# Sliding-window attention feeding a SwiGLU block: key blocks of 64 with four TensorE tiles, against key blocks of 32 with eight

## The chip, the cores and the metric

The kernel runs on one core of a Trainium2 chip. The metric is device time in microseconds (us) for one execution of the whole program. Three runs of the kernel before took 326.04, 326.06 and 326.34 us; the median is 326.06 us.

Engine names follow the profile. PE is TensorE, and PEld is its weight load, which is an instruction of its own ahead of each matmul. DVE is VectorE, ACT is ScalarE, POOL is GpSimd and SP is SyncE. SP and POOL here also issue DMAs.

## The reference

Queries, keys and values are (8 batches, 8 heads, 576 positions, 64 wide). Every query sees itself and the 63 keys before it.

```python
rel = pos[:, None] - pos[None, :]
mask = (rel >= 0) & (rel < 64)
scores = np.where(mask, q @ k.T / 8, -1e9)
attn = softmax(scores)                       # over keys
x = (attn @ v)                               # heads side by side: 4608 tokens x 512
g = x @ w_gate                               # 512 x 1536
out = (g * sigmoid(g) * (x @ w_val)) @ w_out # 1536 x 512
```

The output is 4608 x 512 in float32.

## The kernel before, in words

The 4608 tokens are taken in nine tiles of 512. Tiles 0 to 6 and 8 are the first 512 positions of one batch each; tile 7 (`LAST`) is the last 64 positions of all eight batches. The order of the instructions on each engine is written out by hand, and each engine runs its own list in that order.

One tile has two parts. The attention part gives `xT`, the block's input with the 512 features on partitions. The feed-forward part is 12 gate and value steps (`gate_value`, matmuls on L429) and 4 output projections of 12 matmuls (`project_part`, L438). A gate step is 4 + 4 matmuls of 128x512 into two PSUM banks, a Silu on ACT (L422) and a multiply on DVE (L423) that gives a slice of `hT`. The gate bank alternates between banks 4 and 5, the value bank between 6 and 7, and three `sg` buffers stand between ACT and DVE. The projections of tile t-1 are interleaved with the attention of tile t (main loop at the end of the kernel), so PE has dense work while ACT and DVE handle the attention's softmax.

The attention of a tile from tile 1 on:

- `scores(t, w)` (matmuls on L269) handles four heads, w = 0 or 1. A key block of 64 keys meets the queries of its own block and of the next one, 128 in all. Heads lie as pairs; the half h of the pair is on partitions 64h to 64h+63 (contraction over 64), and the pair x of the two is written to PSUM partitions 64x to 64x+63. So four matmuls, (h, x), use four 64x64 quarters of the PE array. One call makes 32 matmuls: 28 with 128 columns and 4 with 64. In tile 7 a block meets only 64 columns and the call makes 64 matmuls.
- After it, for each h: an exponential on ACT (L282, 960 columns), a multiply by the 0/1 `mask` on DVE (L285), and an addition of the two blocks that one query sees (L290), which gives `both`.
- `sums` (matmuls in `totals`, L302) sums the weights with a matrix of ones, 4 matmuls of 512 columns per w, and ACT takes the reciprocal as exp(-log) (L316, L319).
- `mix` (L369) multiplies values with weights: again 32 matmuls per w in four quarters, 64 in tile 7. `scale` (L385) multiplies by the reciprocal and writes `xT`.

Between these visits PE does projections: visit 1 is `scores(t, 0)`, visit 2 is `scores(t, 1)` with the first `sums`, visit 3 is the second `sums` with `mix`.

Queries and keys come by DMA from POOL (`load_q`, 4 DMAs a tile, 16 in tile 7; `load_k`, 16 DMAs), two tiles ahead of use; values by SP into `v_f`, cast by POOL (`cast_v`). The last tile's values (`load_last_v`, 16 DMAs from POOL) are issued in tile 6. DVE turns queries and keys into the layout with features on partitions (`turn_q` L207, `turn_k` L217) behind gate steps 1, 4, 7 and 10 (6, 7, 9 and 10 in tile 1).

Of the kernel before, what the change touches and what calls it, by code (L numbers as in the profile page):

```python
# [8 lines left out]
P = 128  # L9
# [8 lines left out]
def kernel(  # L18
# [36 lines left out]
    vl = v12[:].rearrange("r g i (c w h) d -> r (g i) c w h d", c=2, w=2)  # L55
    vb = [cst.tile([P, 8, 2, 2, D], BF16, name=f"vb{i}") for i in range(2)]
# [6 lines left out]
    mask = cst.tile([P, 8, 2, 16, 4], BF16, name="mask")  # L63
# [20 lines left out]
    def load_q(t):  # L84

        w = 16 * D - 32
        q_s = stage.tile([P, 4, 16 * D], BF16, name="q_s", tag="q")
        for a, c in quarters:
            p0 = 64 * a + 32 * c
            if t != LAST:  # L90
                nc.gpsimd.dma_start(  # L91
                    q_s[p0:p0 + 32, :, 0:w],
                    q[batch(t), a:H:2, 0:512].rearrange("u (r e) d -> r u (e d)", e=16)
                    [:, :, 32 * c:32 * c + w],
                )
            else:
                for u in range(4):
                    nc.gpsimd.dma_start(  # L98
                        q_s[p0:p0 + 32, u, 0:w],
                        q[:, 2 * u + a, 512:576].rearrange("b (r e) d -> b r (e d)", e=16)  # L100
                        [:, :, 32 * c:32 * c + w],
                    )
        return q_s
# [44 lines left out]
    def load_halves(eng, dst, t, hds=range(H)):  # L148

        for hd in hds:  # L150
            w, x, h = hd // 4, hd // 2 % 2, hd % 2
            eng.dma_start(  # L152
                dst[64 * x:64 * x + 64, :, w, h],
                v[batch(t), hd, 0:512].rearrange("(j r) d -> r j d", r=64),
            )

    def load_last_v():
        for c in range(2):
            for hd in range(H):
                w, x, h = hd // 4, hd // 2 % 2, hd % 2  # L160
                s0 = S - P + 64 * c
                nc.gpsimd.dma_start(
                    vl[64 * x:64 * x + 64, :, c, w, h],
                    v[:, hd, s0:s0 + 64].rearrange("b r d -> r b d"),
                )

    def new_v(t):
        staged[t, "v"] = stage.tile([P, 8, 2, 2, D], FP32, name="v_f", tag="v", bufs=1)

    def stage_v(t):  # L170
        new_v(t)
        load_halves(nc.sync, staged[t, "v"], t)

    def cast_v(t):
        for i in range(4):
            js = slice(2 * i, 2 * i + 2)
            nc.gpsimd.tensor_copy(vb[t % 2][:, js], staged[t, "v"][:, js])  # L177
# [34 lines left out]
    def turn(t, u):  # L212
        turn_q(t, u)
        turn_k(kT[t % 2], staged[t][1], u)

# [31 lines left out]
    quadrants = [(x, h) for h in range(2) for x in range(2)]  # L247

# [3 lines left out]
    def scores(t, w):  # L252

        qT = queries[t]
        s_ps = wide(), wide()
        for j in range(8):
            if t == LAST:
                k_j = kT[t % 2 if j < 4 else 2]
                pieces = [(j, j + 1, 0, k_j, P * (j % 4) + 64),
                          (j, j + 1, 1, k_j, P * (j % 4))]  # L260
            else:
                pieces = [(j, min(8, j + 2), 0, kT[t % 2], 64 * j)]
            for lo, hi, c, src, k0 in pieces:
                for h in range(2):
                    for x in range(2):
                        slot = s_ps[h][half(x)].rearrange("r a b -> r (a b)")
                        n = hi - lo
                        o = P * j + 64 * c
                        nc.tensor.matmul(  # L269
                            slot[:, o:o + 64 * n].rearrange(  # L270
                                "r (n e y) -> r e n y", n=n, e=16
                            ),
                            src[half(h), 2 * w + x, k0:k0 + 64],
                            blocks(qT[half(h), 2 * w + x], t, lo, hi).rearrange(
                                "r e (n y) -> r e n y", n=n
                            ),
                        )
        n = 1024 if t == LAST else 960
        for h in range(2):
            E = eb[2 * w + h]  # L280
            flat = E[:].rearrange("r s z -> r (s z)")[:, 64:64 + n]
            nc.scalar.activation(  # L282
                flat, s_ps[h][:].rearrange("r a b -> r (a b)")[:, 0:n], AF.Exp, scale=0.125
            )
            nc.vector.tensor_mul(  # L285
                flat, flat, mask[:].rearrange("r j c e y -> r (j c e y)")[:, 0:n]
            )
            both = epool.tile([P, 8, 64], BF16, name="both", tag="both")
            lo = 2 if t == LAST else 0
            nc.vector.tensor_add(both[:], E[:, 1:17:2], E[:, lo:lo + 15:2])  # L290
            weights[t, w, h] = E, both
# [7 lines left out]
    def totals(t, w, d):  # L299
        for h in range(2):  # L300
            for x in range(2):
# [3 lines left out]
                    weights[t, w, h][1][half(x)].rearrange("r j (e y) -> r j e y", e=16),  # L305
# [4 lines left out]

    def turned(ap):

        return ap.rearrange("r (e x) -> r x e", e=16)
# [7 lines left out]
    def sums(t, w):  # L321
        d = d_tile(), d_tile()
        totals(t, w, d)
        for x in range(2):
            r = room(1)[:, 0]
            if t == NT - 1:
                log(r.rearrange("r (x e) -> r x e", e=16), turned(d[x]))
            else:
                log(r, d[x])
            invert(r)  # L330
            inverse[t, 2 * w + x] = r

    def sums_wide(t, w):
        d_ps, r = wide(), room(2)
        totals(t, w, (d_ps[:, 0], d_ps[:, 1]))
        for x in range(2):
            inverse[t, 2 * w + x] = r[:, x]
        log(r, d_ps[:])
        invert(r)

# [17 lines left out]
    def mix(t, w, o):  # L358
        E = [weights.pop((t, w, h))[0] for h in range(2)]
        for j in range(8) if t == LAST else (0, 2, 4, 6, 1, 3, 5, 7):  # L360
            if t == LAST:
                pieces = [(j, j + 1, 2 * j + 1 + c, vl[:, j, 1 - c]) for c in range(2)]
            else:
                pieces = [(j, min(8, j + 2), 2 * j + 1, vb[t % 2][:, j])]
            for lo, hi, s0, src in pieces:
                n = hi - lo
                for h in range(2):
                    for x in range(2):
                        nc.tensor.matmul(  # L369
                            blocks(o[x][half(h)], t, lo, hi).rearrange(  # L370
                                "r e (n y) -> r n e y", n=n
                            ),
                            src[half(x), w, h],
                            E[h][half(x), s0:s0 + n].rearrange("r n (e y) -> r n e y", e=16),
                            start=lo == 0 and s0 == 1, stop=lo == 7 and (t != LAST or s0 == 16),
                        )

    def scale(t, u, o_ps):
# [3 lines left out]
        if t == NT - 1:  # L382
            x, o_ps = x.rearrange("r (x e) -> r x e", e=16), turned(o_ps)
            r = r.rearrange("r (x e) -> r x e", e=16)
        nc.vector.tensor_mul(x, o_ps, r)  # L385

    taken = {"a": 0, "g": 0, "v": 0}

    def take(tag):
        taken[tag] += 1  # L390
        return taken[tag] % 2 ^ 1

    def wide():
        return two[take("a")]

    def d_tile():
        return bank[6 + take("v")]

    def mix_all(t):
        tiles = wide(), wide()  # L400
        for w in range(2):
            mix(t, w, (tiles[w][:, 0], tiles[w][:, 1]))
        for u in range(4):
            scale(t, u, tiles[u // 2][:, u % 2])
# [8 lines left out]

    def gate_tiles():
        return out_tile(), d_tile()
# [9 lines left out]
    def gate_value(t, m):  # L425
        pair = gate_tiles()
        for ps, w in zip(pair, (wg, wv)):
            for c in range(4):
                nc.tensor.matmul(  # L429
                    ps[:], w[:, c, P * m:P * m + P], xT[t][:, c, :],  # L430
                    start=(c == 0), stop=(c == 3),
                )
# [10 lines left out]
    def project_end(t, s, o_ps, copy=nc.vector.tensor_copy):  # L443
# [14 lines left out]
        if t == LAST:  # L458
            rows = out.rearrange("(b s) f -> b s f", s=S)[:, 512:S]
            rows = rows.rearrange("b (r e) f -> e b r f", e=16)  # L460
        else:
            rows = rows.rearrange("(r e) f -> e r f", e=16)
        for i in range(4):
            nc.sync.dma_start(rows[4 * s + i], os_[32 * i:32 * i + 32])

    def out_tile():
        return bank[4 + take("g")]

    def project(t, s):
        o_ps = out_tile()  # L470
        project_part(t, (s,), (o_ps,), range(12))
        project_end(t, s, o_ps)

    def project_last(t, s):
        r0 = S * batch(t) + P * s
        os_ = fsb.tile([P, 512], FP32, name="os_", tag="os_", bufs=4)
        for f0, f1 in ((0, 384), (384, 512)):
            o_ps = out_tile()
# [165 lines left out]
    taken["g"] = taken["v"] = 1  # L644
# [38 lines left out]
    tiles = [out_tile(), d_tile(), out_tile(), d_tile()]  # L683
# [5 lines left out]
    scores(1, 0)  # L689
    columns(1, 4)  # L690
    scores(1, 1)
# [81 lines left out]
```

## Time and profile before

| | before |
|---|---|
| median of 3 runs | 326.06 us (326.04 to 326.34) |
| the profiled execution: its own time | 326.34 us |
| its span from first to last instruction | 324.4 us |
| PE busy | 315.9 us, 97% of the span |
| DVE busy | 217.8 us, 67% |
| ACT busy | 167.0 us, 51% |
| POOL busy | 146.3 us, 45% |
| granted TensorE clock | 1.0 |

Busy time is the union of an engine's instructions. Matmuls overlap: a 128x512 matmul lasts 379 ns, but the next one starts about 216 ns later, so the mean duration of one is not its price. The price is the distance between starts, which the chain of waits gives (the stretch of a run of matmuls divided by their number). A few records of matmuls can be missing; the chain then shows an "issue" gap of 0.05 us where nothing stood still.

### The profile page before, as it was taken

Reading aid. Unit: us, or ns where it says so; the run is one execution under the profiler, and the core shown is the slowest. Engines: PE = TensorE matmul, PEld = TensorE weight load, DVE = VectorE, ACT = ScalarE, POOL = GpSimd, SP = SyncE. Lnnn points to the kernel's source line nnn. Section 1 sums busy time; section 2 is a strip of 40 time slices with the busy share of each in tenths; the row PEclk is TensorE's granted clock in tenths of the full one; section 3 lists DMA queues with packets and bytes.
Section 4 is the critical chain, followed back from the end, with each engine's and each line's share of the span. In section 5 each row is a group of like instructions: output and inputs, shape, how many; then the busy total and the mean of one; then the engine's idle time right before and its main releaser. Section 6 shows DMA issues by size and latency. Waiting matters only on the chain.

```text
span 324.4 us, 7013 instructions
## 1 busy us (share of the span) xinstructions
PE 315.9 (97%) x2737; PEld 150.9 (47%) x2780; DVE 217.8 (67%) x345; ACT 167.0 (51%) x239; POOL 146.3 (45%) x260
## 2 busy tenths in 40 slices
PE   7999999999999999999999999999999999999996
PEld 3644444444444444445444544444444544444443
DVE  4764756398676776887678766876687576774422
ACT  5952766337633683358336743565347633773310
POOL 4964766965085794576224999363200000000000
PEclk9999999999999999999999999999999999999999
DMA  7999999998889999949922999599501400021013
GB/s 254 201 196 199 207 154 189 173 172 99 170 156 198 135 171 186 193 58 223 200 34 32 167 182 97 42 197 190 99 3 34 99 2 0 10 85 40 0 25 105
DMA packets 83521, 40.35 MB, mean 124 GB/s; under 512 B 64160, under 2 KB 78752, under 8 KB 83488
## 3 DMA queue, kind: packets, MB, share of 16 engines
q0 software_dynamic: 51488, 22.59, 58.1%
q1 hardware_dynamic: 31456, 16.79, 21.4%
q10 hardware_dynamic: 544, 0.52, 0.5%
q8 instruction: 21, 0.34, 0.4%
q14 instruction: 12, 0.10, 0.1%
HBM read 53.02 MB, written 9.44 MB: 193 GB/s over the span
## 4 chain that ended last, share of the span: by engine, by line
PE 86%; issue 1%; DVE 0%
PE one L429 51%; PE one L438 28%; PE two L269 3%; PE two L369 2%; PE one L302 1%; PE one L480 1%; PE two L302 0%; DVE os__4138 L484 0%
## 5 line engine op out<-in xcount | busy, mean ns | idle before, releaser
L422 ACT ACTIVATE sg<-one 128x512 f32<-128x512 f32 x107 | 63.9, 597 | 112.5 <-PE one L429 86.3
L423 DVE TENSOR_TENSOR hT<-sg,one 128x512 bf16<-128x512 f32 x107 | 74.1, 693 | 60.7 <-PE one L429 59.8
L429 PE MATMUL one<-xT,wg 128*128 128x512 bf16 x414 | 108.1, 379 | 0.9
L429 PE MATMUL one<-xT,wv 128*128 128x512 bf16 x416 | 107.3, 379 | 0.1
L438 PE MATMUL one<-wo,hT 128*128 128x512 bf16 x396 | 93.7, 380 | 2.0 <-issue 0.5
L126 POOL DMA_DIRECT2D k_s<-in_k_dram x112 | 60.7, 567 | 25.0 <-DMA q_s<-in_q_dram 18.1
L429 PEld LDWEIGHTS <-wv 128*128 128x128 bf16 x424 | 41.5, 98 | 50.0
L429 PEld LDWEIGHTS <-wg 128*128 128x128 bf16 x424 | 41.3, 98 | 49.9 <-issue 0.3
L438 PEld LDWEIGHTS <-hT 128*128 128x128 bf16 x420 | 39.0, 98 | 46.6 <-issue 1.8
L282 ACT ACTIVATE eb<-two 128x960 bf16<-128x960 f32 (+1 forms) x32 | 29.5, 974 | 16.5 <-PE two L269 16.4
L217 DVE STREAM_TRANSPOSE kT<-k_s 128x512 bf16<-128x512 bf16 x28 | 36.0, 1286 | 0.0
L285 DVE TENSOR_TENSOR eb<-eb,mask 128x960 bf16<-128x960 bf16 (+1 forms) x32 | 21.1, 659 | 13.0 <-ACT eb L282 13.0
L177 POOL CAST vb<-v_f 128x512 bf16<-128x512 f32 x20 | 11.5, 627 | 34.9 <-DMA out_dram<-os__1184 12.4
L385 DVE TENSOR_TENSOR xT<-two,r 128x512 bf16<-128x512 f32 x34 | 21.7, 685 | 5.7 <-PE two L369 4.8
L319 ACT ACTIVATE r<-r 128x512 f32<-128x512 f32 (+1 forms) x34 | 22.3, 655 | 1.0
L207 DVE STREAM_TRANSPOSE qT<-q_s 128x512 bf16<-128x512 bf16 x32 | 22.2, 700 | 0.2
L316 ACT ACTIVATE r<-one 128x512 f32<-128x512 f32 x31 | 18.3, 591 | 4.7 <-PE one L302 4.7
L91 POOL DMA_DIRECT2D q_s<-in_q_dram x24 | 13.0, 564 | 5.4 <-DVE qT L207 5.4
L290 DVE TENSOR_TENSOR both<-eb 128x512 bf16<-128x512 bf16 x32 | 13.6, 425 | 1.1
L488 ACT ACT_TABLE_LOAD x9 | 11.5, 1283 | 2.0 <-issue 1.9
L152 POOL DMA_DIRECT2D vb<-in_v_dram x16 | 11.3, 723 | 1.9 <-DMA wo<-in_moe_w_out_dram 1.4
L98 POOL DMA_DIRECT2D q_s<-in_q_dram x16 | 8.6, 631 | 7.1 <-DVE qT L207 7.1
(119 smaller groups left out, 191.7 us busy)
## 6 DMA issues: line engine op xcount, KB each, us to landing
k_s<-in_k_dram POOLq DMA_DIRECT2D x112, 56.0 KB, 4.5
q_s<-in_q_dram POOLq DMA_DIRECT2D x24, 248.0 KB, 5.7
v_f<-in_v_dram SPq DMA_DIRECT2D x40, 128.0 KB
wg<-in_moe_w_gate_dram POOLq DMA_DIRECT2D x5, 256.0 KB, 8.1
wv<-in_moe_w_val_dram POOLq DMA_DIRECT2D x5, 256.0 KB, 8.7
q_f<-in_q_dram SPq DMA_DIRECT2D x4, 256.0 KB
wo<-in_moe_w_out_dram POOLq DMA_DIRECT2D x2, 512.0 KB, 9.3
vb<-in_v_dram POOLq DMA_DIRECT2D x16, 64.0 KB, 4.1
```

Of the source, the lines that this page charges most:

```text
L126: nc.gpsimd.dma_start(k_s[p0:p0 + 32, g, :, 0:w], k[b, a:H:2, s:s + P].rearrange("u (r e) d -> r u (e d)", e=4) [:, :, 32 * c:32 * c + w],)
L207: nc.vector.transpose(queries[t][:, u, :].rearrange("r (e x) -> r e x", e=16), staged[t][0][:, u].rearrange("r (e d) -> r e d", d=D)[:, :, ...
L217: nc.vector.transpose(dst[:, u, :].rearrange("r (g x e) -> r g e x", g=4, e=4), k_s[:, :, u].rearrange("r g (e d) -> r g e d", d=D)[:, :, ...
L282: nc.scalar.activation(flat, s_ps[h][:].rearrange("r a b -> r (a b)")[:, 0:n], AF.Exp, scale=0.125)
L285: nc.vector.tensor_mul(flat, flat, mask[:].rearrange("r j c e y -> r (j c e y)")[:, 0:n])
L316: nc.scalar.activation(r, d_ps, AF.Ln)
L319: nc.scalar.activation(r, r, AF.Exp, scale=-1.0)
L385: nc.vector.tensor_mul(x, o_ps, r)
L422: nc.scalar.activation(sg[:], g_ps[:], AF.Silu)
L423: nc.vector.tensor_mul(hT[t][:, m, :], sg[:], v_ps[:])
L429: nc.tensor.matmul(ps[:], w[:, c, P * m:P * m + P], xT[t][:, c, :], start=(c == 0), stop=(c == 3),)
L438: nc.tensor.matmul(o_ps[:], hT[t][:, c, P * s:P * s + P], wo[:, c, :], start=(c == 0), stop=(c == 11),)
```

## The change

Tiles 0 and 1 keep the old scheme (the functions are renamed `scores_second`, `sums_second`, `mix_second`). From tile 2 on:

- A key block has 32 keys and meets 96 queries. Four head pairs u stand on four groups of 32 partitions. Scores contract over 64 (row half h) and write to 32 partitions (column group u): eight tiles of the array, 64x32. Sums and mix contract over 32 (row group u) and write to 64 partitions (column half h): eight tiles, 32x64.
- All eight heads are scored in one visit, `scores(t)`: 18 pieces of 8 matmuls, 144 in all (two of the 16 blocks are cut in two where the query layout breaks). In tile 7: 36 pieces, 288 matmuls. `mix` makes 144 matmuls (256 in tile 7), `sums` 16 of 256 columns.
- Per h there are now two exponentials (960 columns and 512 columns), one multiply over the two masked thirds (`edges`, 1024 elements), and two additions of 512. The reciprocals are two logs and two exponentials of 1024 columns instead of four and four of 512.
- The PSUM banks are named: scores use the two double banks and banks 5 and 7, the projections banks 4 and 6. The first two projections of a tile are copied out by ACT, the others by DVE.
- Gate step 0 goes through its four contraction slices with gate and value alternating.
- Queries are loaded in two halves: 8 DMAs a tile instead of 4, 32 instead of 16 in tile 7. The last tile's values take 32 DMAs instead of 16, issued in tiles 3 and 4. Queries are turned behind gate steps 1 to 4, keys behind 5 to 8; the extra keys of tile 7 behind gate step 0 instead of 8.
- Output rows follow the new order of the queries: the DMAs keep their number and size, only their addresses change.
- In tile 1, behind gate step 2, DVE builds the new mask `edges` (8 small copies, 4 doublings) and clears the borders of `ex` (4 memsets).

The diff, cut to its core:

```diff
+    edges = cst.tile([P, 16, 2, 32], BF16, name="edges")
+    ex = [cst.tile([P, 18, 3, 32], BF16, name=f"ex{i}") for i in range(2)]
...
     def load_q(t):
-        w = 16 * D - 32
+        w = 8 * D - 32
...
+            for g in range(2):
+                run = slice(8 * D * g, 8 * D * g + w)
...
+    def pieces(t, n):
+        if t != LAST:
+            ms = range(n, min(n + 3, 16))
+            groups = [[m for m in ms if m // 8 == g] for g in range(2)]
+            return [(n, [(m, m - n) for m in grp]) for grp in groups if grp]
+        b, c = n // 4, n % 4
+        reach = [(2 * b + i, 2 + i - c) for i in range(2) if 0 <= 2 + i - c < 3]
+        return [(n, reach)]
...
+    def scores(t):
...
+        for n in key_blocks(t):
...
+            for n, reach in pieces(t, n):
...
+                    for h in range(2):
...
+                        for u in range(4):
+                            nc.tensor.matmul(
+                                ps[quarter(u), s0:s0 + step * (k - 1) + 1:step].rearrange(
+                                    "r k (e y) -> r e k y", e=8
+                                ),
+                                src[half(h), u, k0:k0 + 32],
+                                columns_of(qT[half(h), u], reach[i:i + k]).rearrange(
+                                    "r e (k y) -> r e k y", k=k
+                                ),
+                            )
+        for h in range(2):
...
+            nc.vector.tensor_mul(E[:, 2:18, 0:3:2], E[:, 2:18, 0:3:2], edges[:])
...
+            nc.vector.tensor_add(both[:], E[:, 2:18, 0], E[:, far:far + 16, 2])
+            nc.vector.tensor_add(both[:], both[:], E[:, one:one + 16, 1])
...
+    def sums(t):
+        for g in range(2):
+            for h in range(2):
+                for u in range(4):
+                    nc.tensor.matmul(
+                        two[u // 2][half(h), u % 2].rearrange(
+                            "r (g e m y) -> r g m e y", g=2, e=8, m=8
+                        )[:, g],
+                        ones[quarter(u), 0:D],
...
+    def mix(t, o):
...
+        for at, (n, reach) in enumerate(order):
...
+            for h in range(2):
+                for u in range(4):
...
+                    nc.tensor.matmul(
+                        columns_of(o[u][half(h)], reach).rearrange(
+                            "r e (k y) -> r k e y", k=len(ss)
+                        ),
+                        src,
...
     for t in range(1, NT):
         if t > 1:
             set_exp()
-            scores(t, 0)
-            project(t - 1, 0)
+            scores(t)
+            on = bank[4], bank[6]
+            project(t - 1, 0, on[0], on_a)
...
-            o_ps = out_tile()
-            project_part(t - 1, (1,), (o_ps,), range(5))
-            scores(t, 1)
-            sums(t, 0)
-            project_part(t - 1, (1,), (o_ps,), range(5, 12))
-            project_end(t - 1, 1, o_ps)
-            project(t - 1, 2)
-            sums(t, 1)
+            project(t - 1, 1, on[1], on_a)
+            project_part(t - 1, (2,), on[0:1], range(5))
+            sums(t)
+            project_part(t - 1, (2,), on[0:1], range(5, 12))
+            project_end(t - 1, 2, on[0])
             mix_all(t)
-            project(t - 1, 3)
+            project(t - 1, 3, on[1])
...
+        if t in (3, 4):
+            load_last_v(range(4 * t - 12, 4 * t - 8))
...
+            if t == 1 and m == 2:
+                for u in range(4):
+                    a, z = u // 2, 32 * (u % 2)
+                    for i in range(2):
+                        nc.vector.tensor_copy(
+                            edges[quarter(u), 0, i].rearrange("r (e y) -> r e y", e=8),
+                            tri[quarter(u), a ^ i, z:z + 32].rearrange("r (y e) -> r e y", e=8),
+                        )
+                for i in (1, 2, 4, 8):
+                    nc.vector.tensor_copy(edges[:, i:2 * i], edges[:, 0:i])
+                for E in ex:
+                    nc.vector.memset(E[:, 0:2], 0.0)
+                    nc.vector.memset(E[:, 17], 0.0)
+            if 1 <= m < 5 and t + 1 < NT:
+                turn_q(t + 1, m - 1)
+            if 5 <= m < 9 and t + 1 < NT:
+                turn_k(kT[(t + 1) % 2], staged[t + 1][1], m - 5)
+            if m == 0 and 3 <= t < 7:
                 turn_k(kT[2], k_l, t - 3)
```

## The prediction

> **What bounds the kernel now.** I read the page first: busy shares and the chain that ended last.
>
> ```profile
> PE 315.9 (97%) x2737; PEld 150.9 (47%) x2780; DVE 217.8 (67%) x345; ACT 167.0 (51%) x239; POOL 146.3 (45%) x260
> PEclk9999999999999999999999999999999999999999
> PE 86%; issue 1%; DVE 0%
> PE one L429 51%; PE one L438 28%; PE two L269 3%; PE two L369 2%; PE one L302 1%; PE one L480 1%; PE two L302 0%; DVE os__4138 L484 0%
> ```
>
> PE is the bound everywhere, at the full clock, and 79% is dense work (L429, L438) that the change leaves alone. Attention is 6%. So I ask only two things: what PE's attention visits cost afterwards, and whether PE starts to wait. Second, the chain in order of time, for tile 4 and then tile 7:
>
> ```profile
> 140.76 0.55 PE two L269 x30
> ...
> 145.09 0.55 PE two L269 x32
> 145.63 0.22 PE one L302 x4
> ...
> 150.06 0.34 PE one L302 x4
> 150.40 0.84 PE two L369 x64
> ...
> 242.45 0.64 PE two L269 x57
> ...
> 246.87 0.64 PE two L269 x63
> 247.51 0.22 PE one L302 x3
> ...
> 251.93 0.34 PE one L302 x4
> 252.27 1.18 PE two L369 x128
> ```
>
> A normal tile spends 0.55 + 0.55 + 0.22 + 0.34 + 0.84 = 2.50 us on attention, tile 7 spends 0.64 + 0.64 + 0.22 + 0.34 + 1.18 = 3.02. More than 2.5 us a tile cannot be won. Third, how fast small matmuls start (timeline rows: start, stretch; then two stretches of tile 7's mix, with how many were under way in each):
>
> ```profile
> 140.69 0.62 PE L269 MATMUL two<-qT,kT 64*64 64x128 bf16 x32
> 150.23 1.01 PE L369 MATMUL two<-eb,vb 64*64 64x128 bf16 x64
> 242.38 0.71 PE L269 MATMUL two<-qT,kT 64*64 64x64 bf16 x64
> 252.10 1.35 PE L369 MATMUL two<-eb,v 64*64 64x64 bf16 x128
> 252.60:252.85 0.25, 0.25 (x50) 1.00 0.46 115
> 252.60:253.25 0.65, 0.65 (x95) 1.00 0.49 123
> ```
>
> A stretch ends one duration (0.19 us) after the last start. With 128 columns: (1.01 - 0.19)/63 = 13.0 ns per matmul, four at a time, so 52 ns a group against 128/512 of the 216 ns of a dense matmul = 54 ns: the array's columns bound it. With 64 columns the columns would allow 6.8 ns, but scores take (0.71 - 0.19)/63 = 8.2 and mix (1.35 - 0.19)/127 = 9.1; inside the mix 95 - 50 = 45 start in 0.40 us, 8.9 ns. I read that as a limit on how fast PE gets through a pair of weight load and matmul.
>
> **The change, part by part.**
>
> *Scores and mix, tiles 2 to 6 and 8.* Columns per group fall: 18 groups of eight at a mean of 80 columns, against 8 groups of four at 120 per call, two calls. By columns a visit would be 18 x (80/512 x 216 = 34 ns) = 0.61 us. But it now has 144 pairs where scores and mix had 64 each. Price p per matmul: the lower end is the columns' 34/8 = 4.2 ns; the upper end is 9.1. I take 8.2, the row nearest in kind (scores, many short matmuls in a row, no wait among them): eight tiles help the columns, not the rate of pairs. Entering and leaving a visit costs 0.55 - (0.62 - 0.19) = 0.12 us. Scores 144 x 8.2 + 120 = 1.30 us, mix the same.
>
> *Sums.* 8 matmuls of 512 columns, four at a time, become 16 of 256, eight at a time: two groups of 108 ns + 0.12 for a visit of its own = 0.34 us, against 0.22 + 0.34.
>
> Together 1.30 + 1.30 + 0.34 = 2.94 against 2.50: +0.44 us, six tiles +2.6 us.
>
> *Tile 7.* Scores 288 x 8.2 + 120 = 2.48, mix 256 x 8.2 + 120 = 2.22, sums 0.34: 5.04 against 3.02, +2.0 us.
>
> All seven tiles as one formula: 6 x 288 + 544 = 2272 matmuls, so the PE part is 2.272 p - 14.0 us (p in ns; 14.0 = 6 x (2.50 - 0.58) + 3.02 - 0.58). p = 8.2 gives +4.6, p = 9.1 gives +6.7.
>
> The Trainium skill (TensorE: Matmul & The Clock Gate, Part 3, "The mechanism") has matmuls on different tiles start about 4 ns apart. By it eight start within 32 ns and the columns would bound; that is the first rival below. The 8.2 and 9.1 ns rows, on four different tiles, do not show it for a long run.
>
> *New mask in tile 1.* DVE gets extra work behind gate step 2. Rows:
>
> ```profile
> 57.53 0.69 DVE L423 TENSOR_TENSOR hT<-sg,one 128x512 bf16<-128x512 f32 x1 [1.04 <-PE one L429]
> L654 DVE COPY mask<-tri 64x64 bf16<-64x64 bf16 x4 | 0.7, 208 | 0.0
> L659 DVE COPY mask<-mask 128x128 bf16<-128x128 bf16 (+2 forms) x3 | 1.0, 340 | 0.1
> L661 DVE MEMSET eb<- 128x32 uint32 x4 | 0.2, 85 | 0.0
> ```
>
> 8 small copies x 0.21 + 4 doublings (0.2, then 0.50, 0.23, 0.29) + 4 memsets x 0.085 = 3.2 us. DVE is free at 58.2, so it ends at 61.4; `turn_q` (0.70) and step 3's multiply (0.69) end at 62.8. Step 5's value half, which overwrites that bank, begins at 61.58 in the trace: PE waits 1.2 us. DVE stays behind, and the four key turns at steps 5 to 8 (1.29 + 0.69 = 1.98 against 1.73 us a step) cost it 0.25 each: about 0.3 us more. I take +1.5; the ends are 0.2 (copies at the 112 ns of the smallest memset, L537) and 1.9.
>
> *What I cost at nothing, and its cover.* (a) From tile 2 on the key turns put DVE about 1.1 us behind; a multiply may end 2.6 - 1.0 = 1.6 us late before PE's bank is missed, so 0.5 us is left. (b) Sums wait for the softmax: table load ends 1.1 us after gate end, exponentials 2 x (0.97 + 0.59) = 3.1, then DVE 0.66 x 1024/960 + 2 x 0.43 = 1.6: 5.8 us, while PE has 1.30 + 29 x 0.216 = 7.6. Cover 1.8. (c) Mix overwrites bank `two0`, so it waits for the first log: about 0.5 + 1.01 after sums begin, against 0.34 + 7 x 0.216 = 1.85. Cover 0.3, the thinnest; if gone, it adds its lateness in each of seven tiles. (d) ACT's two copies (0.59) sit between exponentials and logs, ACT being idle there. (e) POOL: 4 more issues a tile x 0.54 = 2.2 us, 16 more in tile 7's load, and 32 value issues (0.77) in tiles 3 and 4 (12 us each) delay the casts and key loads queued behind them. POOL ends tile 3's list at 137 and tile 5's loads at 192 in the trace; pushed back some 20 us they still land ahead of use at 222. In tile 1 queries come first and land by about 52, their turn is at 56; key DMAs wait there for query DMAs to land, as they do now, so the last lands near 62 as now, and is wanted after 65. (f) SP: value loads wait for POOL's casts with output DMAs behind them; four `os_` buffers cover it. (g) Gate step 0's order waits less for `scale`, which is already hidden.
>
> **Sum.** 2.6 + 2.0 + 1.5 = 6.1 us. The profiled execution took 326.34 us (span 324.4, 1.9 around it), 0.28 above the median; from the median of 326.06 I get 332.2. Own range of this case: the first 28 pairs of a visit at column speed save 14 x 28 x (8.2 - 4.2) ns = 1.6, and the mask may cost only 0.2: 6.1 - 1.6 - 1.3 = 3.2, so 329.3 (28 is an estimate: 24 of tile 7's mix start in its first 0.18 us, before the slower pace). With p = 9.1 and 1.9: 6.7 + 1.9 = 8.6: 334.7.
>
> **The rivals.**
>
> *Columns bound (faster).* If pairs can start as fast as the columns allow, p is 4.2 in normal tiles and about 2.4 in tile 7 (43 to 48 columns a group): 1.728 x 4.2 + 0.544 x 2.4 - 14.0 = -5.4, plus the mask 1.5: -3.9, so 322.2. Place: the long visits; the sign turns where 2.272 p = 14.0 - 1.5, at p = 5.5 ns. For it: 128-column groups do run at column speed. Against: both 64-column rows. 13%. Between 5.5 and 7 ns, 326 to 329.5: 8%.
>
> *Softmax late for sums.* If DVE's strided multiply and additions run at half speed (3.1 us per h), the second half ends 1.3 us after PE wants it: 7 x 1.3 = 9 us more, 341. Against: L290's strided halves take 0.43 us for 512, in line with L285's 0.66 for 960. 6%.
>
> *Tiles do not overlap.* One matmul at a time would cost 34 ns each: 2.272 x 34 - 14.0 = +63, 390 us. The rows above speak against it: 13 ns for 128 columns. 1%. The Trainium skill (TensorEngine Tiling (Array Packing), "Instruction Overhead") gives about 60 cycles per matmul and warns against splitting a dimension that is already small; 25 ns each, an estimate from it, would give 369 us, and the trace shows a third of that price.
>
> **How the numbers follow.** Forecast 72%: 332.2, own range 329.3 to 334.7. No change means within 0.2% (0.65 us), about what this measurement can tell. Range 326.0 to 337.0: it leaves out the column-bound case (13%) and the late softmax (6%). Faster: the column-bound case, 13%. Same: the low end of the in-between case, 5%. Slower: 82%.
>
> **What would show it.** Right: chain stretches of about 1.3 us for each scores and mix visit, 2.2 to 2.5 us in tile 7, about 8 ns per matmul; a gap of PE near gate step 5 of tile 1, ended by DVE. Wrong: visits of 0.75 us (columns bind), PE waiting for DVE or ACT ahead of L412's sums or L481's mix, or a key turn in tile 1 that waits for a DMA.

## The result, and the profile after

The changed kernel takes 341.18 us (median of four runs, 339.60 to 341.85) against 326.20 us beside it (326.04 to 326.64). The ratio is 1.045, 95% interval 1.0412 to 1.0488: slower, and beyond the predicted range. The profiled execution took 341.85 us (span 340.1), 15.5 us more than that of before. These lines are from its page (busy time, granted clock, the DMA queues, shares of the chain):

```profile
PE 324.3 (95%) x4041; PEld 158.2 (47%) x4084; DVE 204.2 (60%) x333; ACT 165.3 (49%) x225; POOL 176.5 (52%) x316
PEclk9999999999999999999999999999979599999999
q8 instruction: 32, 0.52, 0.7%
PE 83%; issue 3%; DVE 1%; ACT 0%; DVEq 0%
```

PE is still the bound, but two things are new in tile 7, the slices around 250 and 265 us: the clock digit falls to 7 and 5, and the chain holds 3% "issue", time in which PE waited for nothing that the profile shows. Queue q8 brings instructions, in 32 transfers of 16 KB. Before it had 21:

```profile
q8 instruction: 21, 0.34, 0.4%
```

The changed kernel has 4084 PE matmuls and as many weight loads, the one before 2780. Together that is 8168 and 5560 instructions, or 31.9 and 21.7 times 256, so q8's transfers go with PE's list in blocks of 256.

The chain in order of time puts a price on each tile. Tile 4:

```profile
142.67 0.91 PE two L342 x94
143.57 0.40 PE one L342 x46
...
144.35 5.99 PE one L550 x27
150.34 0.35 PE two L412 x16
150.69 1.40 PE one L550 x6
```

The scores take 0.91 + 0.40 = 1.31 us in one visit, the sums 0.35, and PE waits for nobody. The same view for tile 7:

```profile
246.07 1.46 PE two L342 x162
247.53 2.58 issue
...
251.83 0.22 issue
252.04 7.22 PE one L550 x27
...
263.09 2.33 issue
...
266.34 4.90 PE one L550 x11
```

Counted by their starts, PE stops inside the scores after 167 of 288 matmuls, for 2.58 us, and inside the mix after 211 of 256, for 2.33 us. Behind the stops the projections on L550 are slow: 7.22 us for 27 matmuls that take 5.99 in tile 4, 4.90 for 11 that take 2.54. The table by stretches of the same execution (start and end in us, length, PE busy with its matmuls, granted clock, DMA share, GB/s) says why:

```profile
247.50:250.10 2.60, 0.03 (x4) 1.00 0.00 0
251.20:254.60 3.40, 3.18 (x18) 0.51 0.02 5
263.10:265.40 2.30, 0.00 (x0) 0.86 0.26 61
265.50:271.20 5.70, 5.37 (x57) 0.50 0.05 13
```

The clock is halved for 3.4 us behind the first stop and for about 6 us behind the second. In the first stop the DMA engines are nearly idle, and the whole traffic of 246 to 251 us is one packet, 0.02 MB on queue q8, in the DMA view of that window:

```profile
q8 instruction: 1, 0.02, 1.7%
```

No data moved; what arrived was a block of instructions. The trace has it start at 247.22 us, 0.3 us before PE stops, and PE goes on at 250.11.

Where the 15.5 us are, from one gate end to the next in the two chains: 0.77 up to tile 2's scores, 3.55 in tiles 2 to 6 and 8 (0.67, 0.47, 0.47, 0.49, 0.75, 0.70), 11.71 in tile 7, and -0.52 at the end and outside the span. Tile 7's 11.71 are 4.91 of stops, about 4.7 of half clock (7.22 against 5.99 and 4.90 against 2.54, and an estimated 1.1 in the short stretches beside them), and, as what is left, about 2.1 of work.

### The profile page after: what moved, and what is told of

It is laid out like the page before. It is cut to its first block, busy times and chain, and to the rows that moved or that the text cites. A ratio compares the mean times of both kernels' runs of the same rounds, so it can differ in the third digit from the quotient of the medians.

```text
span 340.1 us, 9664 instructions
## 1 busy us (share of the span) xinstructions
PE 324.3 (95%) x4041; PEld 158.2 (47%) x4084; DVE 204.2 (60%) x333; ACT 165.3 (49%) x225; POOL 176.5 (52%) x316
## 4 chain that ended last, share of the span: by engine, by line
PE 83%; issue 3%; DVE 1%; ACT 0%; DVEq 0%
PE one L541 47%; PE one L550 27%; PE two L342 2%; PE one L481 2%; PE two L481 1%; PE one L342 1%; PE one L590 1%; PE two L412 1%; DVE hT L533 0%; DVE edges L847 0%; PE two L270 0%; PE two L457 0%; PE two L378 0%; DVE edges L852 0%; ACT os__879 L557 0%
## 5 line engine op out<-in xcount | busy, mean ns | idle before, releaser
L541 PE MATMUL one<-xT,wv 128*128 128x512 bf16 x416 | 112.4, 379 | 1.1 <-DVE hT L533 0.3
L550 PE MATMUL one<-wo,hT 128*128 128x512 bf16 x396 | 95.3, 391 | 2.6 <-issue 1.8
L550 PEld LDWEIGHTS <-hT 128*128 128x128 bf16 x420 | 40.0, 100 | 48.8 <-issue 6.6
L222 DVE STREAM_TRANSPOSE kT<-k_s 128x512 bf16<-128x512 bf16 x28 | 36.4, 1301 | 0.1
L96 POOL DMA_DIRECT2D q_s<-in_q_dram x48 | 25.9, 562 | 1.0 <-DMA vb<-in_v_dram 0.6
L174 POOL DMA_DIRECT2D v<-in_v_dram x32 | 18.3, 578 | 5.9 <-DMA k_s<-in_k_dram 3.7
L395 ACT ACTIVATE r<-two 128x1024 f32<-128x1024 f32 (+1 forms) x17 | 16.8, 990 | 7.7 <-PE two L412 6.1
L362 DVE TENSOR_TENSOR ex<-ex,edges 128x1024 bf16<-128x1024 bf16 x14 | 10.3, 739 | 16.0 <-ACT ex L359 16.0
L398 ACT ACTIVATE r<-r 128x1024 f32<-128x1024 f32 (+1 forms) x20 | 19.4, 972 | 0.6
L103 POOL DMA_DIRECT2D q_s<-in_q_dram x32 | 18.1, 576 | 0.0
L498 DVE TENSOR_TENSOR xT<-one,r 128x512 bf16<-128x512 f32 x16 | 10.3, 686 | 9.7 <-PE two L481 9.1
L355 ACT ACTIVATE ex<-two 128x960 bf16<-128x960 f32 (+1 forms) x14 | 13.7, 982 | 3.6 <-PE two L342 3.5
L498 DVE TENSOR_TENSOR xT<-two,r 128x512 bf16<-128x512 f32 x20 | 12.7, 680 | 3.8 <-PE two L457 3.8
L342 PEld LDWEIGHTS <-kT 64*32 64x32 bf16 x1152 | 10.1, 89 | 5.7 <-issue 5.7
```

The source lines that it names most:

```text
L96: nc.gpsimd.dma_start(q_s[p0:p0 + 32, :, run], q[batch(t), a:H:2, 256 * g:256 * g + 256] .rearrange("u (r e) d -> r u (e d)", e=8)[:, :, 3 ...
L174: nc.gpsimd.dma_start(vl[quarter(hd // 2), c, :, hd % 2], v[:, hd, s0:s0 + 32].rearrange("b r d -> r b d"),)
L222: nc.vector.transpose(dst[:, u, :].rearrange("r (g x e) -> r g e x", g=4, e=4), k_s[:, :, u].rearrange("r g (e d) -> r g e d", d=D)[:, :, ...
L342: nc.tensor.matmul(ps[quarter(u), s0:s0 + step * (k - 1) + 1:step].rearrange("r k (e y) -> r e k y", e=8), src[half(h), u, k0:k0 + 32], co ...
L398: nc.scalar.activation(r, r, AF.Exp, scale=-1.0)
L541: nc.tensor.matmul(pair[i], (wg, wv)[i][:, c, P * m:P * m + P], xT[t][:, c, :], start=(c == 0), stop=(c == 3),)
```

## The experiments

**Theory A**, from that packet: PE's instructions (weight loads and matmuls count alike; a pair is one of each) come in blocks of 256. Entering one block asks for the next, which is usable some 3.6 us later. Dense work spends 256 instructions in 128 x 0.216 = 27.6 us and never notices. A run of short pairs spends them in 1.07 us, so a run that holds two block ends must stop. Counted in the program's order from PE's first weight load, tile 7's scores begin at instruction 5745, and the first matmul behind the stop is instruction 6080 = 24 x 256 - 64. Behind the mix stop it is 6848 = 27 x 256 - 64. So both stops lie 64 instructions ahead of a multiple of 256, which is called a block's end here. If PE's program has 64 instructions ahead of those that the trace lists, the stops lie at the end itself; no run decides that, and the argument needs only that the place in the block is the same. The rivals: B, tile 7 waits for its data; C, eight tiles at once lower the clock by themselves, or the number of short pairs does. Apart from this, the price in normal tiles: pairs or columns.

### Moving the block ends

The diff is that of the first version; the second has 32 in place of 64.

```diff
     keep_warm(6)
+    for _ in range(64):
+        nc.tensor.matmul(warm[0:D, 0:16], ones[:, 0:D], ones[:, 0:16])
```

> The changed kernel with 64 tiny warm-up pairs (128 TensorE instructions) at the very start, where PE is idle; nothing else differs. Theory A: half a block of shift. Tile 7's first stop moves from after 168 of its 288 scores matmuls to after about 232 of them, its second from after 212 of 256 mix matmuls to after about 148; both still about 2.4 us, no stop over 0.3 us in another tile; time 340 to 343 us. Theory B (data of tile 7 late): the stops stay after 168 and 212, since what they wait for is the same instruction. Theory C (clock by itself): no stop moves.

Measured: 341.31 and 342.15 us. The chain of tile 7 (scores from 249.83 us on, mix from 262.82):

```profile
251.81 2.08 issue
253.88 0.60 PE one L342 x53
254.49 6.37 PE one L550 x29
...
264.14 1.84 issue
```

Counted by starts, the stops now come after 231 of the scores' matmuls and 147 of the mix's: where A had them, with the same data and the same work. B and C fall, for they had no reason to move. One thing in the expectation was wrong: PE is not idle at the start. The 64 pairs took 3.58 us there, 56 ns each, and tile 2's scores begin 4.2 us later; that the total stayed is shorter stops (3.92 us in place of 4.91) and one half-clock stretch in place of two.

> The changed kernel with 32 tiny warm-up pairs (64 TensorE instructions) at the very start, where PE waits for its first data anyway; nothing else differs, every later wait and every piece of work is the same. Theory A (TensorE's instructions come in blocks of 256; entering one block asks for the next, which is there about 3.5 us later; a run of more than 256 short instructions gets through a block in 1.07 us and stops 64 instructions before the block's end): all block ends move by 64 instructions, and then nearly every attention visit holds one. I count nine block ends that come too early (one each in the mix of tiles 2, 4, 6, 8, one each in the scores of tiles 3 and 5, two in the scores of tile 7, one in its mix): nine stops of about 2.4 us, 22 us in place of 5.3, and after most of them 1.7 to 3.4 us lost to half clock. Time 365 to 385 us against 341. Theory B (tile 7 waits for its data, its values or queries or the softmax): stops where they were, after 168 and 212 matmuls, time 341 to 342. Theory C (the clock falls by itself because of eight tiles at once): no new stops, 341 to 342.

Measured: 343.03 and 348.34 us, with mean clocks of 0.995 and 0.985; the trace is that of the second. The stops in its chain:

```profile
87.02 0.67 issue
112.62 0.64 issue
226.99 1.62 issue
256.26 2.05 issue
270.19 2.29 issue
```

Normal tiles now stop too: in the mix of tiles 2 (87.02) and 6 (226.99) and the scores of tile 3 (112.62), and, too short for this list of longest pieces, in the mix of tiles 4 (0.50) and 8 (0.15), each after 131 to 135 matmuls. That is where A puts block ends, and no rival has stops there. But A's size was far off. The scores of tile 5 lost 0.08 us, and the end after 135 matmuls of tile 7's scores nothing; the stops sum to 7.9 us and not 22. The trace shows why: for the stop at 87.02 the block's transfer starts at 84.90, 0.8 us before the mix itself, while PE still is in dense work. So in dense work the request goes out earlier than my count had it, and there every eight instructions are 0.86 us gained. How many instructions ahead was not measured. In place of "usable 3.5 us after entry" the traces give a firmer figure: in the sixteen stops of over 0.4 us that I compared with the transfers, PE went on 2.3 to 3.2 us after the start of a 16 KB transfer that itself took 0.9 to 1.6 us.

### The same run of pairs in the kernel before, whole and in quarters

The diff is that of the whole run; the other version has 72 pairs each at steps 2, 4, 6 and 8.

```diff
         for m in range(12):
+            if t == 5 and m == 6:
+                for i in range(288 // 4):
+                    for h in range(2):
+                        for x in range(2):
+                            nc.tensor.matmul(
+                                two[0][half(x), h, 0:64], identb[half(h), half(h)],
+                                ones[half(h), 0:64],
+                            )
             gate_value(t, m)
```

> The kernel before, its attention unchanged on four tiles, with 288 extra matmuls of 64 columns on those four tiles (288 weight loads and 288 matmuls) in one run ahead of gate step 6 of tile 5; their result is used by nothing. No data has to come for them. Theory A (a block of 256 instructions is asked for when the one ahead of it is entered and is there 3.6 to 3.8 us later, a run of short pairs gets through it in 1.07 us): one stop of 2.4 to 2.7 us inside the extra run, with half clock behind it that costs 0, 1.7 or 3.4 us. Pairs 288 x 8.2 to 9.1 ns = 2.4 to 2.6 us; time 326.3 + 2.5 + 2.5 + 1.7 = 333 us, 331 to 335. Theory B (the stops in the changed kernel's tile 7 were waits for its data) and theory C (it takes eight tiles at once): no stop, 326.3 + 2.5 = 328.8 us, 328.5 to 329.2.

> The kernel before with the same 288 extra matmuls, in four runs of 72 ahead of gate steps 2, 4, 6 and 8 of tile 5, some 5 us of dense matmuls between two runs. Theory A: a run of 144 instructions is shorter than a block and the next block is there long before the next run: no stop, full clock, 2.5 us of pairs and four times some 0.12 us to enter and leave a run: 326.3 + 3.0 = 329.3 us, 328.8 to 329.8. If it were the number of short pairs as such that stops TensorE or lowers its clock: the same as in one run, 331 to 335.

Measured: with the 288 pairs in one piece 334.12 us (331.75 to 334.63), ratio 1.0215 (1.017 to 1.0259) to the kernel before at 326.47; cut into four 329.09, 329.24 and 329.51 us, ratio 1.0086 (1.0069 to 1.0103). The profiled execution of the cut one took 852 us, with dense matmuls about 600 ns apart from end to end; why is open, and neither its time nor its trace is used. The chain of the first:

```profile
196.94 2.37 PE one L429 x11
199.31 1.63 PE two L740 x183
200.94 3.04 issue
203.98 1.61 PE two L740 x80
205.59 1.55 PE one L429 x4
```

Old kernel, four tiles, constant operands that lay there long before, and the stop is there: 3.04 us after 183 pairs. That is A's place by the count above (15 x 256 - 64). The table by stretches has the clock at 0.50 behind it:

```profile
201.00:203.90 2.90, 0.00 (x0) 0.90 1.55 101
204.00:205.50 1.50, 1.50 (x105) 0.50 1.59 101
205.60:209.00 3.40, 3.40 (x14) 0.83 0.43 30
```

The same 288 pairs cut into four cost 329.24 - 326.47 = 2.8 us, as expected of pairs at 8.2 to 9.1 ns and four more visits with no stop; for want of a trace this half rests on the times. So it is neither eight tiles, nor tile 7's data, nor the number of pairs: it is their density.

### Tile 7 in halves

`scores` and `mix` get an argument for the half: key blocks 0 to 15 or 16 to 31, the first or the last 16 of the mix's pieces.

```diff
-            scores(t)
+            scores(t, 1 if t == LAST else None)
...
+            if t == LAST:
+                o = bank[5], bank[7], two[0][:, 0], two[0][:, 1]
+                mix(t, o, 0)
+                project_part(t - 1, (3,), on[1:2], range(6))
+                mix(t, o, 1)
...
         for m in range(12):
+            if t + 1 == LAST and m == 10:
+                scores(LAST, 0)
             gate_value(t, m)
```

> The changed kernel with tile 7's scores in two halves of 144 matmuls (the first ahead of gate step 10 of tile 6, the second where all of them stood) and its mix in two halves of 128 with six projection matmuls between; the same work and the same number of instructions. Theory A: no burst is longer than 288 instructions, with 1.3 us or more of dense work between two. The stop in the scores goes, the one in the mix shrinks from 2.5 to about 1.2 us, about 1 us can be left in dense work behind the second half; where a stop is short the clock may stay up. Tile 7 loses about 2 to 5 us in place of 11.7: time 331 to 336 us. Theory B: the second half of the scores waits for the same data, time 339 to 341. Theory C (eight tiles at once lower the clock): the same 544 matmuls give the same lost clock, about 341.

Measured: 335.64 us (334.41 to 336.68), ratio 1.0266 (1.0238 to 1.0294), within A's 331 to 336. Nothing was removed but the length of two runs, and 5.5 us went. The remaining stops stand where A left them:

```profile
249.09 1.62 PE one L556 x7
250.70 0.59 issue
...
261.46 1.21 issue
```

0.59 us in dense work behind the second half of the scores (two blocks had been spent too fast), and 1.21 in the second half of the mix. A wait of its own came with the cut: the first half now stands too early for a key turn, and PE waits 0.27 us for DVE (L222) after three matmuls. That one is data.

### Pairs or columns: half the columns, and half the pairs

```diff
-                                ),
+                                )[:, 0:4],
                                 src[half(h), u, k0:k0 + 32],
...
-                two[h][:, :, 0:wide_n], AF.Exp, scale=0.125,
+                two[h][:, :, 0:wide_n], AF.Exp, scale=0.0,
...
-                        ),
+                        )[:, :, 0:4],
                         src,
```

> The changed kernel with scores and mix of tiles 2 to 8 on half of their columns (4 of 8 in the e direction; the other half of the scores and of the weighted sum is left out, and the exponent is taken of 0). As many pairs, half the columns. If pairs set the speed of a visit (8.33 ns for a weight load and its matmul, as read in the changed kernel): a normal visit's scores still take 1.19 us from first to last start, the mix 1.20, and time and stops stay, 340 to 343 us. If columns set it (18 groups of 80 columns at 34 ns = 0.61 us a visit would have been the bound, so that 1.19 us is columns plus contention): a visit falls by 0.3 us or more, 14 visits and tile 7's two double ones by 5 us in all, 336 us or less.

Measured: 339.04 and 340.21 us. The timeline of tile 4's scores (start, stretch, tiles' shape), first in the changed kernel, then with half the columns:

```profile
142.60 0.97 PE L342 MATMUL two<-qT,kT 64*32 64x96 bf16 x96
143.37 0.60 PE L342 MATMUL one<-qT,kT 64*32 64x96 bf16 x48
```

```profile
142.21 0.94 PE L342 MATMUL two<-qT,kT 64*32 64x48 bf16 x96
142.96 0.59 PE L342 MATMUL one<-qT,kT 64*32 64x48 bf16 x48
```

From first to last start 1.17 us in place of 1.19, the mix 1.18 in place of 1.20. Columns are not the price. The 8.33 ns are also not the least distance between two starts: in tile 4's scores of the changed kernel the first 32 matmuls start 3 to 4 ns apart inside each group of eight, and only after a gap of 78 ns does every further one start 8 to 9 ns behind the one ahead. That speaks for the supply of instructions as the limit of a long run, 4.17 ns each, but no run tries it apart. The stops in tile 7 stayed after 167 and 211 matmuls, at 2.05 and 2.15 us, 0.7 us less in sum than in the changed kernel's trace.

```diff
     def mix(t, o):
...
-                for u in range(4):
+                for u in range(2):
```

> The changed kernel with the mix of tiles 2 to 8 for head pairs 0 and 1 alone (half of its matmuls, 72 of 144 and in tile 7 128 of 256, each with its 96 columns; the weighted sum of the other heads is left out). It has half the columns too, but where the version with half the columns kept all pairs, here the pairs go, and only four tiles of the array take turns. Theory 1 (the price is 8.33 ns per pair, whichever tile): from first to last start 71 x 8.33 = 0.59 us in place of 1.20. Theory 2 (the price is that of a round, 66.7 ns until the same tile can start again, with 96 columns or 48): 1.15 to 1.20 us as before, since there are still 18 rounds. On the blocks of 256 instructions (theory A): a tile now has 752 PE instructions, so block ends fall elsewhere: a stop after 136 of 144 matmuls in tile 5's scores (0.1 to 2 us), one after 144 of 288 in tile 7's scores (2 to 2.7 us), perhaps a small one after 128 in tile 4's, and none in any mix, tile 7's included. If the stops were waits for data: after 168 in tile 7's scores, and one in its mix. Time: 326.4 + 0.8 - 0.8 (six tiles) + 0.4 (tile 7) + 3.5 (stops) + 1.7 to 3.4 (half clock) = 332 to 334 us.

Measured: 332.39 and 332.57 us, as A's sum had it. The mix has 72 matmuls in 0.70 us from first to last start (the changed kernel 144 in 1.20): neither theory's number, but the round of 66.7 ns is out. The pace is 9.9 ns per pair, four tiles taking turns; 96 columns at the 216 ns of 512 make 40 ns a round of four, 10 ns each, so with four tiles the columns may bind again, an estimate for the twelve rounds with all 96 columns that was not tried. The block ends were moved a third time:

```profile
210.46 0.34 PE one L342 x38
210.80 0.51 issue
...
245.88 0.56 PE one L342 x62
246.45 2.50 issue
```

Tile 5's scores stop after 135 matmuls as foretold, and no mix stops, tile 7's included. In tile 7's scores PE lost 0.05 us at the block end after 143 matmuls, where I had expected the stop, and 2.50 at the next, after 271. That agrees with the finding of the 64 moved instructions: the earlier end's block had been asked for in dense work.

### The mask spread out

```diff
-            if t == 1 and m == 2:
-                for u in range(4):
+            if t == 1 and m in (0, 9):
+                for u in range(2 * (m // 9), 2 * (m // 9) + 2):
...
+            if t == 1 and m == 10:
                 for i in (1, 2, 4, 8):
...
+            if t == 1 and m == 11:
                 for E in ex:
```

> The changed kernel with the mask's build spread over tile 1's gate steps: four of the eight copies behind step 0, four behind step 9, the doublings behind step 10, the memsets behind step 11, in place of all behind step 2. If the prediction's step on the new mask holds in kind (a burst of DVE work that makes PE wait for hT and for a free bank): the 0.77 us that PE lost in tile 1 goes, tile 7 keeps its two stops (half clock and the length of a stop alone make +-1.5 us): 341.2 - 0.8 = 340.4 us, 339 to 341.2. If those 0.77 us were something else (transposes, a load): 341.2.

Measured: 339.83 us (339.24 to 340.80), ratio 1.0412 (1.0387 to 1.0438) against 1.045 (1.0412 to 1.0488): a gain in the expected size, not told from none by the times. The chain of tile 1 tells it. First the changed kernel, then the spread mask:

```profile
51.47 0.58 ACT os__879 L557
52.05 0.50 ACT os__883 L557
...
52.59 5.14 PE one L541 x23
...
59.71 0.31 DVE edges L852
...
62.35 10.74 PE one L541 x49
```

```profile
51.82 0.58 ACT os__879 L557
52.41 0.50 ACT os__883 L557
...
52.95 20.66 PE one L541 x95
73.61 0.91 PE two L342 x94
```

With the mask spread PE goes through tile 1's twelve gate steps in one piece, 20.66 us; with the mask in one place they last from 52.59 to 73.74, 21.15. So the mask cost 0.49 us, not 0.77. The rest stands in both chains ahead of the gate steps: PE waits for ACT's two copies of tile 0's output banks and begins tile 1's steps at 52.59 and 52.95, where the kernel before begins them at 52.09 without that wait.

### All of it together

```diff
-    keep_warm(6)
+    for i in range(66):
+        a = half(i % 2)
+        nc.tensor.matmul(warm[a, 0:16], ones[a, 0:D], ones[a, 0:16])
```

with the halves and the spread mask.

> The changed kernel with tile 7's scores and mix in halves, the mask's build spread, and 66 tiny warm-up pairs on two tiles in place of the six wide warm-up matmuls at the start (120 instructions more, about the same 2.5 us while PE has no data). Theory A: with block ends moved by 120 instructions no block end falls where it comes too early but one, in the second half of tile 7's mix: one stop of 1.2 to 1.4 us in place of 5.3, half clock behind it 0 to 1.7. Time: 326.3 + 3.6 (six normal tiles) + 1.5 to 2 (tile 7's pairs and its extra visits) + 1.3 + 0 to 1.7 = 332.7 to 335, I take 333.5. If alignment had nothing to do with it: as the version with halves alone, less 0.8 for the mask, 334.8.

Measured: 334.56 us (333.94 to 334.67), ratio 1.0244 (1.0228 to 1.026). One long stop is left, 1.23 us in the second half of tile 7's mix, at the foretold place, and the clock stays up behind it. But 334.8 was the number for "alignment has nothing to do with it", so the time alone decides nothing here. It is the best that this scheme gave, 8 us behind the kernel before. Of these the stop is 1.2 us, and another 1.2 lie ahead of tile 2's scores (at 74.14 us in its chain, at 72.97 in that of before); most of the rest is the work of the added pairs.

## Why the prediction was wrong, and where it was right

Slower was the forecast, 332.2 us; the time is 9 us beyond it, nearly all from one step.

**Normal tiles, right.** The step "Scores 144 x 8.2 + 120 = 1.30 us, mix the same" measured 1.31 in the chain, at 8.33 ns per pair; sums 0.35 for 0.34. Against +0.44 us a tile, tiles 3, 4 and 5 have +0.47 to +0.49. Tiles 2 and 6 have 0.2 to 0.3 more; their gate steps hold small stops 64 instructions ahead of a multiple of 256, which is A's place, though this was not tried apart. Tile 8 has 0.2 more from a gap inside its mix, which is there in every version with the whole mix and stays open. Six tiles: 3.55 for 2.6.

**Tile 7, wrong.** The step that failed is "Scores 288 x 8.2 + 120 = 2.48, mix 256 x 8.2 + 120 = 2.22 ... +2.0 us". The price of a pair held for the first 167, and then there were no instructions. The prediction took p from runs of at most 128 pairs, 256 instructions, which hold one block end and did not stop, and carried it to runs of 288 and 256 pairs, which hold two each. What is left for the work is about 2.1 us, as forecast; 4.9 of stops and 4.7 of half clock were on no line of the sum and in no rival. What could have been seen: the page of before lists 21 instruction transfers of 16 KB, and the change adds 1304 pairs to PE's list, most of them in runs of 288 instructions and more.

**The half clock is a consequence, and not of every stop.** In the traces of the changed kernel and of the experiments it began at or behind thirteen of the fifteen stops of 1.2 us or more, the shortest of 1.21 us and the longest of 3.04; it did not follow one of 2.08 and one of 1.23, and none of the shorter ones. So the time of one and the same kernel varies: the changed kernel's 339.60 has a mean clock of 0.994, its 341.85 one of 0.985. The Trainium skill (TensorE: Matmul & The Clock Gate, "What's actually happening") has a free-running window of about 3.4 us that decides between half and full clock. The half-clock stretch of 3.4 us agrees with it. The Trainium skill's table in that section asks for an idle window of that length before the clock falls; here stops of 1.21 to 3.04 us were enough, and the measurement decides.

**The rule that the case needed.** The Trainium skill (Runtime: NRT & Kernel Launch, "Instruction fetch mechanics") says that instructions come in 16 KiB blocks of 256, fetched while the block ahead executes, at a cost that is "mostly hidden". The blocks and the fetch agree with the 32 transfers of 16 KB and with the moved stops. "Hidden" nearly holds in dense work, but not in these runs: at 4.17 ns per instruction a block lasts 1.07 us, and PE went on 2.3 to 3.2 us after the transfer's start.

**The mask, right in kind, too large.** "+1.5" is the mis-sized term: 0.49 by the spread mask. The 0.50 beside it is a cover that failed: gate step 0 waits in tile 1 for ACT's copies. The prediction had that step's new order as "already hidden", from `scale`; that the alternating order, which needs both banks at once, makes the wait is argued from the diff and was not tried.

**The rivals.** Columns bound: refuted, half the columns left a visit at 1.17 us of 1.19, and the prediction's formula for p carries the normal tiles. Softmax late, 341 us: the sum fits, the mechanism does not; the chain has PE work right up to L412's sums and L481's mix, with no DVE or ACT between. Tiles that don't overlap: refuted by 8.33 ns per pair, where 34 would be needed. The covers (a) to (c) held, (c) too: the mix follows the sums' seven projections without a wait.

## What to carry to other kernels

Count the instructions of PE's runs as well as its nanoseconds: where more than about 256 short ones stand in a row, look whether the next block can be there, and cut the run with dense work (5.5 us here for moving two halves). A stop marked "issue" in the middle of equal matmuls, with one instruction packet beside it, is this; instructions added at the program's start (here 64 and 128) tell it from a data wait, because the stops move. And a change that trades wide matmuls for more narrow ones pays per pair: here 144 pairs at 8.33 ns, with all their columns and with half.

## What the runs showed of the hardware that was not expected

- In a long run a weight load and its matmul cost 8.33 ns on eight tiles, 4.17 ns an instruction, unchanged when the columns were halved; the first 32 matmuls of a run start faster, 3 to 4 ns apart inside a group of eight.
- PE's instruction supply: blocks of 256; stops at the same place in the block, 64 instructions ahead of a multiple of 256, in every kernel whose block ends were moved (by 64, by 128, and by the half mix); 2.3 to 3.2 us from the start of a transfer to the next matmul.
- A stop's place depends on everything ahead of it in PE's program. Added instructions that change nothing else moved stops into tiles that had none (7.9 us in all against 4.9).
- Half clock for 3.4 us, once about twice that, at or behind thirteen of fifteen stops of 1.2 to 3.0 us.
